# Reordering a recurrent-attention kernel with a fused feed-forward: output pieces between input pieces, preparation in three lots, one VectorE copy for two transposed tiles, input rows left in place

## The chip, the cores and the metric

The kernel runs on one core of a Trainium2 chip. A core has five engines that run their own instruction queues: TensorE (PE; its weight loads are listed apart as PEld), VectorE (DVE), ScalarE (ACT), GpSimd (POOL) and SyncE (SP, which here only issues DMA transfers). The metric is the device time of one execution in microseconds; three runs of the kernel before gave a median of 331.74 us.

## The reference

```
for t in range(S):                                   # S = 768, 4 batches, 8 heads, head size 40
    y[t]  = einsum('bhd,bhde->bhe', r[t], state)
    Sa    = einsum('bhde,bhe->bhd', state, a[t])
    state = state * w[t][:, :, None, :] - outer(Sa, b[t]) + outer(v[t], k[t])
x = y as [3072 tokens, 320]                          # all heads of a token side by side
out = (relu(x @ w_in) ** 2) @ w_out                  # 320 -> 2048 -> 320
```

A recurrence over 768 tokens for 32 (batch, head) pairs, then a feed-forward layer with squared ReLU on the result. Inputs and output are float32; the kernel computes with bf16 operands and float32 sums.

## The kernel before, in words

The 768 tokens are cut into 6 **chunks** of 128. In a chunk the 32 (batch, head) pairs are worked off in 8 **stages** of four pairs each (two heads side by side on the 128 partitions, times two), so there are 48 stages, numbered `st` = 0 to 47, and two stages share one batch of one chunk (`m` = 0 to 23). Chunks are tied by the state `UZ`, but the eight stages of a chunk are independent, so the loop is a hand-written software pipeline over `st`. There is no scheduler: each engine executes its instructions in the order in which this Python code emits them, and a wait holds everything behind it on that engine.

A stage consists of these steps (names as in the profile):

- `st_a_mm` / `st_a_ev`: PE forms two 128x128 products per pair into the PSUM banks `ca0`, `ca1`; two DVE instructions mask them into `CN`.
- `st_p` / `st_m`: PE forms `P` (from the state `UZ` and from `CN`), ACT copies it to `Mc`. Then two corrections on PE, `st_corr` (both on the line of the matmuls `P<-Mc,CN` and `P<-c,CN`), with DVE's `c` between them (`st_c1`). `st_sn` on ACT writes the result Sa into `EVX` (called Sn below; in the profile `EVX<-P`), then squares `CN` for a norm (`jk`); POOL adds up `x` and `Cc` for a later check.
- `st_t`: PE transposes Sa, and the state of the stage two back, into one PSUM tile `tb`; DVE copies the first half to `SnT`, ACT the second half to `UBD`.
- `st_ex_mm` / `st_ex_ev`: in the next stage PE forms `ex0`, `ex1` from `RV` and `SnT`; two DVE instructions mask them into `EVX`.
- `st_z`, `st_kb`: PE forms `uy` from `UBD` and from `EVX` with K and B; `st_y`, two stages on, writes the output `YS` and the new state `UZ` on DVE.

**Preparation of a batch `m`** is spread over earlier stages by a table of (stage offset, lot): `prep_cast` (ACT's Ln of w, three POOL casts), `prep_decay` (PE's running sum `cs`, two ACT exponentials `GI` and `Gp`, the products K and B with `GI` on POOL), `prep_rv`, `prep_kb`, `prep_ga` (eight PE transposes each into a PSUM tile `t`, then copies out: `RV` and `KBT` on ACT; `GT` on ACT and from it `AT` on DVE). `load` issues six DMA transfers per batch on SP; four batches fit into the buffers.

**The feed-forward** is cut in pieces that fill PE between the steps. Half a chunk (256 tokens) gives eight input pieces (`ffn_in`: six matmuls `hp`, ReLU on ACT to `hs`, the square `Gt` on DVE or POOL) and four output pieces (`ffn_out`: eight matmuls `op_`; after each second piece an ACT copy `osb` and a DMA to the output). `filler(st)` is called three times per stage and emits one waiting piece each time, so four stages take the twelve pieces of a half chunk. Before the input pieces, `gather` copies all eight heads' rows from `YS` into `X` with eight DMA transfers. After the loop, `while fill` emits what is left. At the end of each chunk two ACT squares `jm` over `Mc` and `Cc` sum the check energies.

At the very end the kernel reads a flag and would run a slow general path if the check failed.

Of the kernel before, what the change touches and what calls it, by code (L numbers as in the profile page):

```python
# [18 lines left out]
def kernel(  # L19
# [71 lines left out]
    NACC = NS + 2 * NCH + 2 * NBC  # L91
    AN, AM, AC, AG, AI = 0, NS, NS + NCH, NS + 2 * NCH, NS + 2 * NCH + NBC
# [31 lines left out]
    for key, n in (("R", 2), ("V", 2), ("A", 2), ("G", 2), ("K", 4), ("B", 4)):  # L124
        pads[key] = []
        for i in range(n):
            t_ = gl.tile([128, NHH, 64], BF16, name=f"{key}p{i}")
            nc.vector.memset(t_[:, :, D:64], 0.0)
            pads[key].append(t_)
    GTs, RVs = [], []  # L130
    for i in range(4):
        t_ = gl.tile([128, PB, L + 2], BF16, name=f"GT{i}")
        nc.vector.memset(t_[:, :, 0:1], 1.0)
        GTs.append(t_)
        t_ = gl.tile([128, 2, PB, LV], BF16, name=f"RV{i}")
        nc.vector.memset(t_[:, :, :, L:LV], 0.0)
        for s in range(2):
            o_ = 64 * s
            nc.vector.tensor_copy(
                out=t_[o_:o_ + D, 0, :, L:LV],  # L140
                in_=IDb[o_:o_ + D, o_:o_ + D].rearrange("p (u d) -> p u d", u=1)
                .to_broadcast([D, PB, D]))
        RVs.append(t_)
    EVXs = []
    for i in range(NEV):
        t_ = gl.tile([128, 2, 2, EV], BF16, name=f"EVX{i}")
        nc.vector.memset(t_[:, :, :, 2 * LV:EV], 0.0)
        EVXs.append(t_)
    UZs = []
# [14 lines left out]
    def prep_cast(m):  # L164
        o = bt[m] = Batch()
        o.R, o.A, o.G, o.V = (pads[key][m % 2] for key in "RAGV")
        o.K, o.B = (pads[key][m % 4] for key in "KB")
        o.GT, o.RV = GTs[m % 4], RVs[m % 4]
        o.EVX = [EVXs[(2 * m + u) % NEV] for u in range(2)]
        o.lnW = ffp.tile([128, NHH * D], FP32, name="lnW", tag="lnW", bufs=2)  # L170
        nc.scalar.activation(out=o.lnW[:], in_=nat.pop(("W", m))[:].rearrange("p h e -> p (h e)"),
                             func=ACTF.Ln)
        for key, pad in (("A", o.A), ("V", o.V), ("R", o.R)):
            nc.gpsimd.tensor_copy(out=pad[:, :, 0:D], in_=nat.pop((key, m))[:])

    def prep_decay(m):
# [7 lines left out]
        nc.scalar.activation(out=o.G[:, :, 0:D], in_=cs[:], func=ACTF.Exp,  # L184
                             accum_out=ACC[:, AG + m:AG + m + 1])
        for key, pad in (("K", o.K), ("B", o.B)):
            eng = nc.vector if m < 2 and key == "B" else nc.gpsimd
            eng.tensor_tensor(out=pad[:, :, 0:D], in0=nat.pop((key, m))[:], in1=GI[:],  # L188
                                    op=ALU.mult)

    def prep_load(m):
        load(m)

    def transposes(dst, pad):
        for j in range(PB):
            src = pad[:, 2 * j:2 * j + 2, :].rearrange("p a b -> p (a b)")
            nc.tensor.transpose(out=dst[:, j, :], in_=src, identity=IDb[:])  # L197

    def prep_rv(m):
        o = bt[m]  # L200
        t1 = ps.tile([128, 2, PB, L], BF16, name="t1", tag="ff", bufs=2)
        transposes(t1[:, 0], o.R)
        transposes(t1[:, 1], o.V)
        nc.scalar.activation(out=o.RV[:, :, :, 0:L], in_=t1[:], func=ACTF.Copy)  # L204
# [28 lines left out]
    CNs, Ps, SnTs, uys, Mc, Cc, YSs = {}, {}, {}, {}, {}, {}, {}  # L233
# [58 lines left out]
    def st_sn(st):  # L292
# [11 lines left out]
        if q == NQ - 1:  # L304
            for src, at in ((Mc.pop(c), AM), (Cc.pop(c), AC)):
                jm = qdp.tile([128, NQ, 4, D], BF16, name="jm", tag="jm", bufs=1)
                nc.scalar.activation(out=jm[:], in_=src[:], func=ACTF.Square,  # L307
                                     accum_out=ACC[:, at + c:at + c + 1])

    def st_t(st, su):  # L310
# [13 lines left out]
        if st < NS:  # L324
            SnT = SnTs[st] = qdp.tile([128, 2, L], BF16, name="SnT", tag="SnT")
            nc.vector.tensor_copy(out=SnT[:], in_=tb[:, 0:2])  # L326
        if 0 <= su < NS - NQ:
            nc.scalar.activation(out=UBD[:, 2 * q:2 * q + 2, :], in_=tb[:, 2:4], func=ACTF.Copy)

    exs = {}  # L330

    def st_ex_mm(st):
# [4 lines left out]
        for u in range(2):  # L337
            for i in range(2):
                for s in range(2):
                    lhsT = SnT[half(s), i, :] if u else o.RV[half(s), 1, j0 + i, 0:L]  # L340
# [4 lines left out]
    def st_ex_ev(st):
        EVX = EVXs[st % NEV]
        ex = exs.pop(st)
        for s in range(2):
            nc.vector.tensor_tensor(  # L349
                out=EVX[:, :, s, 0:2 * LV].rearrange("p i (u x) -> p i u x", u=2)[:, :, :, 0:L],  # L350
                in0=ex[s][:], in1=MEX[:].rearrange("p (i u) x -> p i u x", u=2), op=ALU.mult)

    def st_z(st):
        c, o, j0, p2, EVX = where(st)
        uy = uys[st] = ps.tile([128, 2, LV], FP32, name="uy", tag="uy")
        if c > 0:
            for i in range(2):
                nc.tensor.matmul(out=uy[:, i, :], lhsT=UBD[:, p2.start + i, :],
                                 rhs=o.RV[:, 0, j0 + i, :], start=(i == 0), stop=False,
                                 skip_group_check=True)  # L360

    def st_kb(st):
        c, o, j0, p2, EVX = where(st)
        uy = uys[st]
        for u, key in ((0, o.K), (1, o.B)):
            for i in range(2):
                for s in range(2):
                    nc.tensor.matmul(out=uy[half(s), i, :], lhsT=key[:, 2 * (j0 + i) + s, :],  # L368
# [51 lines left out]
    def ffn_in(c, hf, jj):  # L420
        flush()
# [3 lines left out]
        for u in range(2):  # L425
            j = 2 * jj + u
            for g in range(3):
                nc.tensor.matmul(out=hp[:, u, :], lhsT=WIN[g][0:rows[g], j * 128:(j + 1) * 128],  # L428
                                 rhs=Xs[c, hf][g][0:rows[g]].rearrange("p a b -> p (a b)"),
# [238 lines left out]
```

## Time and profile before

| | |
|---|---|
| median of 3 runs (range) | 331.74 us (331.05 to 333.25) |
| the profiled execution's own time | 330.49 us |
| its span (first to last instruction) | 328.8 us |
| mean granted PE clock | 0.943 of full |

The times below are microseconds from the start of that span. In timeline rows the first number is the start, the second the duration of a group of instructions, and square brackets name the idle time of the engine just before it and what ended it. Consecutive instructions of one engine overlap a little, so start-to-start distances are used where a queue is added up.

### The profile page before, as it was taken

What the parts mean: (1) busy time and instruction counts of PE and PEld (TensorE: products, weight loads), DVE (VectorE), ACT (ScalarE), POOL (GpSimd) and SP (SyncE); (2) the same over time, 40 slices, a digit from 0 to 9 for tenths busy, and PEclk for the clock granted to TensorE, in tenths of its full rate; (3) what the DMA queues carried; (4) which work ended last, traced back from release to release, by engine and by line L of the source; (5) the groups of instructions that cost most, each with busy time, mean ns of one, the idle gap of its engine ahead of it and who ended that gap; (6) DMA issues with size and microseconds to landing.
All of it is one profiled execution on the core that took longest, in us unless ns stands there. A gap on an engine that the chain in (4) does not pass through costs nothing.

```text
span 328.8 us, 10009 instructions
## 1 busy us (share of the span) xinstructions
PE 280.4 (85%) x3856; PEld 213.3 (65%) x3856; DVE 222.7 (68%) x545; ACT 232.8 (71%) x569; POOL 188.3 (57%) x342
## 2 busy tenths in 40 slices
PE   4478777799999799999799999899998899888990
PEld 3446555577777577777577777677776677666770
DVE  7226968587787587786686886686876775954430
ACT  3366766886886986887986787886887886538450
POOL 3367757296585485676476676476674673533300
PEclk9555978899999999999999999999999999999997
DMA  8992999985737437635736844735862701000100
GB/s 136 174 165 40 176 165 167 169 126 99 151 71 138 94 69 141 126 69 112 128 55 121 147 82 78 144 62 120 131 106 47 147 18 44 20 23 28 55 22 29
DMA packets 164187, 32.86 MB, mean 100 GB/s; under 512 B 158660, under 2 KB 163780, under 8 KB 164130
## 3 DMA queue, kind: packets, MB, share of 16 engines
q1 hardware_dynamic: 161586, 29.44, 49.7%
q0 software_dynamic: 2544, 2.68, 5.1%
q8 instruction: 32, 0.52, 0.7%
q14 instruction: 25, 0.20, 0.2%
HBM read 28.84 MB, written 3.93 MB: 100 GB/s over the span
## 4 chain that ended last, share of the span: by engine, by line
PE 56%; ACT 18%; issue 7%; DVE 7%; POOL 4%; DMA 3%; SPq 3%; ACTq 0%; DVEq 0%; POOLq 0%
PE hp L428 12%; PE t L197 6%; PE ex L341 4%; PE P L280 4%; PE cs L179 4%; ACT hs L433 3%; ACT jm L307 3%; PE uy L368 3%; ACT RV L204 3%; SPq L81 3%; PE tb L316 3%; PE ca L242 2%; DMA NV<-in_v_dram 2%; DVE c L288 2%; ACT GT L224 2%
## 5 line engine op out<-in xcount | busy, mean ns | idle before, releaser
L428 PE MATMUL hp<-X,WIN 120*128 120x256 bf16 (+1 forms) x576 | 78.9, 275 | 8.1 <-ACT osb L458 6.1
L433 ACT ACTIVATE hs<-hp 128x512 bf16<-128x512 f32 x96 | 57.3, 597 | 26.1 <-PE hp L428 22.7
L349 DVE TENSOR_TENSOR EVX<-ex,MEX 128x512 bf16<-128x512 f32 x96 | 61.8, 686 | 1.7 <-PE ex L341 0.5
L428 PEld LDWEIGHTS <-WIN 120*128 120x128 bf16 (+1 forms) x576 | 50.7, 98 | 18.9 <-issue 9.6
L250 DVE TENSOR_TENSOR CN<-ca,MCN 128x512 bf16<-128x512 f32 x96 | 61.4, 681 | 0.7 <-PE ca L242 0.7
L299 POOL TENSOR_TENSOR x<-Mc,c 128x160 f32<-128x160 bf16 x48 | 23.3, 486 | 66.7 <-DVE c L288 66.6
L436 POOL TENSOR_TENSOR Gt<-hs 128x512 bf16<-128x512 bf16 x43 | 48.4, 1125 | 9.9 <-ACT hs L433 9.6
L454 PEld LDWEIGHTS <-Gt 128*128 128x128 bf16 x384 | 34.3, 97 | 13.4 <-POOL Gt L436 0.8
L280 PEld LDWEIGHTS <-CN 128*128 128x128 bf16 x384 | 23.2, 98 | 27.2 <-issue 23.6
L326 DVE COPY SnT<-tb 128x256 bf16<-128x256 bf16 x48 | 14.0, 291 | 33.3 <-PE tb L322 27.6
L300 POOL TENSOR_TENSOR Cc<-x,EVX 128x160 bf16<-128x160 f32 x48 | 25.3, 527 | 17.1 <-ACT EVX L296 16.8
L436 DVE TENSOR_TENSOR Gt<-hs 128x512 bf16<-128x512 bf16 x53 | 27.4, 519 | 9.4 <-ACT hs L433 9.2
L225 DVE TENSOR_TENSOR AT<-t,GT 128x512 bf16<-128x512 bf16 x24 | 10.2, 425 | 31.4 <-ACT GT L224 31.4
L302 ACT ACTIVATE jk<-CN 128x512 bf16<-128x512 bf16 x48 | 30.1, 627 | 0.0
L212 ACT ACTIVATE KBT<-t 128x1024 bf16<-128x1024 bf16 x24 | 24.6, 1024 | 6.0 <-PE t L197 6.0
L204 ACT ACTIVATE RV<-t 128x1024 bf16<-128x1024 bf16 x24 | 24.6, 1023 | 5.1 <-PE t L197 3.0
L188 POOL TENSOR_TENSOR Kp<-NK,GI 128x320 bf16<-128x320 f32 x24 | 22.4, 933 | 6.6 <-ACT GI L182 5.6
L280 PE MATMUL P<-c,CN 128*128 128x40 bf16 x192 | 12.4, 181 | 13.5 <-DVE c L288 13.5
L288 DVE TENSOR_TENSOR c<-P,Mc 128x160 bf16<-128x160 f32 x48 | 15.3, 319 | 10.4 <-PE P L280 9.6
L378 DVE TENSOR_TENSOR YS<-uy,GT 128x256 bf16<-128x256 f32 x48 | 20.2, 421 | 1.2 <-PE uy L368 0.8
L242 PE MATMUL ca<-AT,KBT 64*128 64x128 bf16 x384 | 20.0, 228 | 1.2 <-DVE AT L225 1.2
L296 ACT ACTIVATE EVX<-P 128x160 bf16<-128x160 f32 x48 | 14.4, 300 | 8.7 <-PE P L280 8.4
(142 smaller groups left out, 636.6 us busy)
## 6 DMA issues: line engine op xcount, KB each, us to landing
NW<-in_w_dram SPq DMA_DIRECT2D x24, 160.0 KB
NK<-in_k_dram SPq DMA_DIRECT2D x24, 160.0 KB
NB<-in_b_dram SPq DMA_DIRECT2D x24, 160.0 KB
NA<-in_a_dram SPq DMA_DIRECT2D x24, 160.0 KB
NV<-in_v_dram SPq DMA_DIRECT2D x24, 160.0 KB
NR<-in_r_dram SPq DMA_DIRECT2D x24, 160.0 KB
out_dram<-osb SPq DMA_DIRECT2D x24, 160.0 KB
X<-YS SPq DMA_DIRECT2D x93, 20.0 KB
```

The source lines that it names most:

```text
L204: nc.scalar.activation(out=o.RV[:, :, :, 0:L], in_=t1[:], func=ACTF.Copy)
L212: nc.scalar.activation(out=o.KBT[:], in_=t2[:], func=ACTF.Copy)
L242: nc.tensor.matmul(out=ca[s][:, i, u, :], lhsT=o.KBT[half(s), u, j0 + i, :], rhs=o.AT[half(s), j0 + i, :], start=(i == 0 and u == 0), stop ...
L250: nc.vector.tensor_tensor(out=CN[:, :, s], in0=ca[s][:], in1=MCN[:], op=ALU.mult)
L280: nc.tensor.matmul(out=P[:, i, s, 0:D], lhsT=CN[:, i, s, 1, :], rhs=X[:, 2 * i + s], start=False, stop=last, skip_group_check=True)
L300: nc.gpsimd.tensor_tensor(out=Cc[c][:, q], in0=t_[:], in1=Sn, op=ALU.add)
L302: nc.scalar.activation(out=jk[:], in_=CN[:, :, :, 1, :], func=ACTF.Square, accum_out=ACC[:, AN + st:AN + st + 1])
L349: nc.vector.tensor_tensor(out=EVX[:, :, s, 0:2 * LV].rearrange("p i (u x) -> p i u x", u=2)[:, :, :, 0:L], in0=ex[s][:], in1=MEX[:].rearra ...
L428: nc.tensor.matmul(out=hp[:, u, :], lhsT=WIN[g][0:rows[g], j * 128:(j + 1) * 128], rhs=Xs[c, hf][g][0:rows[g]].rearrange("p a b -> p (a b) ...
L433: nc.scalar.activation(out=hs[:], in_=hp[:].rearrange("p u x -> p (u x)"), func=ACTF.Relu)
L436: later.append(lambda: eng.tensor_tensor(out=Gt[:, 2 * jj:2 * jj + 2].rearrange("p j a b -> p (j a b)"), in0=hs[:], in1=hs[:], op=ALU.mult))
L454: nc.tensor.matmul(out=op_[:], lhsT=Gts[c, hf][:, j, b_, :], rhs=WOUT[:, j, :], start=(j == 0), stop=(j == NJ - 1))
```

## The change

1. **Feed-forward order.** A half chunk's four output pieces no longer follow its own eight input pieces; they are emitted between the input pieces of the next half chunk (two outputs, four inputs, two outputs, four inputs). Pieces of a half chunk may start two stages after its gather (three before). In stages 44 and later a fourth `filler` call is made.
2. **Squares.** Of eight squares `Gt`, six go to POOL and two to DVE (four and four before); POOL's are emitted at once, not deferred.
3. **Preparation in three lots.** Ln, casts and decay of batch `m` come in stage 2m-3, K/B and G/A transposes together in stage 2m-2, R/V in stage 2m-1 (before: 2m-4, 2m-3, 2m-2). Loads are issued at 2m-9 (before 2m-7). Before the loop the work of batch 1 is cut down, K's product with `GI` comes ahead of the casts, and part of the constants is written later (`more_constants`), while three more large memsets come early.
4. **Copies.** `RV` (`RVT` now) is copied from PSUM by DVE, not ACT. `SnT` and `UBD` become one tile `TB`, copied by one DVE instruction. R/V and G/A transposes use the PSUM bank `ex0`.
5. **Order in a stage.** `st_p` comes ahead of the first filler; the two `ex` evictions are split around `c`; `st_t` comes before the decay sum and before `st_kb`.
6. **Input rows in place.** PE reads `YS` directly; only the two heads that do not fit into the first three row groups are moved, by four small DMAs (eight and a buffer `X` before). The weight `WIN` is loaded in ten pieces in this row order, over stages 1 to 3.
7. **Energies.** The two `jm` per chunk become four of half the size, in later stages.

```diff
-        t1 = ps.tile([128, 2, PB, L], BF16, name="t1", tag="ff", bufs=2)
...
-        nc.scalar.activation(out=o.RV[:, :, :, 0:L], in_=t1[:], func=ACTF.Copy)
+        t1 = turned(o.RV, tag="ex0")
+        nc.vector.tensor_copy(out=o.RVT[:, :, :, 0:L], in_=t1[:])
...
-            nc.vector.tensor_copy(out=SnT[:], in_=tb[:, 0:2])
...
-            nc.scalar.activation(out=UBD[:, 2 * q:2 * q + 2, :], in_=tb[:, 2:4], func=ACTF.Copy)
+            nc.vector.tensor_copy(out=TB[:, lo:hi], in_=tb[:, lo:hi])
...
-        eng = nc.gpsimd if jj % 2 and not tail else nc.vector
+        eng = nc.gpsimd if jj % (NJ // 4) and not tail else nc.vector
+        if jj % (NJ // 4) or tail:
+            flush()
...
+            order = outs[:2] + ins[:4] + outs[2:] + ins[4:]
...
+                ((-3, 1, prep_ln), (-3, 1, prep_cast), (-3, 4, prep_decay), (-2, 1, prep_kb),
+                 (-2, 1, prep_ga), (-1, 1, prep_rv)))
```

The loop body after the change, where the order of the steps stands:

```
        if st + 1 < NS:  st_a_mm(st + 1)
        if 1 < st <= NS: st_ex_mm(st - 1)
        if st < NS:      st_p(st); st_m(st)
        if st >= 2:      st_y(st - 2)
        if 1 <= st <= NS: st_ex_ev(st - 1, 0)
        filler(st)
        st_z(st - 1); st_corr(st, Mc, False); st_c1(st)
        st_ex_ev(st - 1, 1); st_a_ev(st + 1)
        filler(st)
        prepare(st, 1)
        st_corr(st, c1s[st], True); st_sn(st)
        filler(st)
        st_t(st, st - 2); flush()
        prepare(st, 4)
        if st >= NS - 4: filler(st)
        st_energy(st - NQ // 2)
        st_kb(st - 1)
        ...
```

Three places in the order. First ACT in the steady state, where the names are those of the steps above. Before, two stages in a row, the first with the G/A transposes (`GT`), the second with R/V and K/B:

```order
L273 ACTIVATE Mc<-P 128x160
L224 ACTIVATE GT_215<-t_2576 128x4x128
L171 ACTIVATE lnW<-NW 128x320
L433 ACTIVATE hs<-hp 128x512
L296 ACTIVATE EVX_227<-P 128x4x40
L302 ACTIVATE jk,ACC<-CN 128x512
L182 ACTIVATE GI,ACC<-cs 128x320
L184 ACTIVATE Gp_183,ACC<-cs 128x8x40
L328 ACTIVATE UBD<-tb 128x256
```

After, the stage with K/B and G/A:

```order
L275 ACTIVATE Mc<-P 128x160
L443 ACTIVATE hs<-hp 128x512 x2
L216 ACTIVATE KBT<-tt 128x1024
L226 ACTIVATE GT_190<-tt 128x4x128
L298 ACTIVATE EVX_201<-P 128x4x40
L304 ACTIVATE jk,ACC<-CN 128x512
L443 ACTIVATE hs<-hp 128x512
L314 ACTIVATE jm,ACC<-Mc 128x640
```

In the changed order two ReLUs, `KBT` and `GT` stand between `Mc` and Sn (`EVX<-P`); before, `GT`, Ln and one ReLU did. `UBD` and `RV` are gone from ACT.

Second, DVE after the change in a stage with R/V, from `c` to the first instruction of the next stage:

```order
L290 TENSOR_TENSOR c_4830<-P,Mc 128x160
L354 TENSOR_TENSOR EVX_203<-ex_4793,MEX 128x2x2x128
L252 TENSOR_TENSOR CN<-ca_4782,MCN 128x2x256
L252 TENSOR_TENSOR CN<-ca_4783,MCN 128x2x256
L210 COPY RV_195<-tt 128x8x128
L334 COPY TB<-tb 128x512
L445 TENSOR_TENSOR Gt<-hs 128x512
L383 TENSOR_TENSOR YS<-uy,GT_190 128x256
```

The copies of `RV` and of the whole `tb` now stand in DVE's queue behind the `CN` evictions; before, a copy of half of `tb` (`SnT`) stood there alone.

Third, POOL before the first stage. Before:

```order
L174 CAST Ap_179<-NA 128x8x40
L174 CAST Vp_175<-NV 128x8x40
L174 CAST Rp_171<-NR 128x8x40
L188 TENSOR_TENSOR Kp_187<-NK,GI 128x8x40
L217 COPY EVX_227<-Vp_175 128x4x40
```

After:

```order
L144 MEMSET UZ_206 128x2048
L144 MEMSET WIN_209 128x2048
L195 TENSOR_TENSOR KBp_179<-NK,GI 128x8x40
L181 CAST GAp_175<-NA 128x8x40
L181 CAST RVp_171<-NV 128x8x40
L181 CAST RVp_171<-NR 128x8x40
```

K's product (`Kp`, `KBp` now) moved ahead of the three casts, and two memsets moved ahead of it.

More of the change, by code (lines that the diff above doesn't have):

```diff
@@ L131 @@
     for i in range(4):
[L132 to L142, printed above, removed]
@@ L143 @@
-        RVs.append(t_)
-    EVXs = []
+        GTs.append(gl.tile([128, PB, L + 2], BF16, name=f"GT{i}"))
+        nc.gpsimd.memset(GTs[i][:, :, 0:1], 1.0)
+        RVs.append(gl.tile([128, 2, PB, LV], BF16, name=f"RV{i}"))
     for i in range(NEV):
[L146 to L149, printed above, removed]
+        EVXs.append(gl.tile([128, 2, 2, EV], BF16, name=f"EVX{i}"))
     for i in range(2):
         UZs.append(gl.tile([128, NP, 128], BF16, name=f"UZ{i}"))
-    UBD = gl.tile([128, NP, 128], BF16, name="UBD")
+    for g in range(PB - 1):
+        WIN.append(gl.tile([128, DFF], BF16, name=f"WIN{g}"))
@@ new lines, with more_constants @@
+    for t_, eng in ((UZs[1], nc.gpsimd), (WIN[2], nc.gpsimd), (WIN[0], nc.vector),
+                    (WIN[1], nc.vector)):
+        eng.memset(t_[:], 0.0)
+    def more_constants():
+        for t_ in RVs:
+            nc.vector.memset(t_[:, :, :, L:LV], 0.0)
+            for s in range(2):
+                o_ = 64 * s
+                nc.vector.tensor_copy(
+                    out=t_[o_:o_ + D, 0, :, L:LV],
+                    in_=IDb[o_:o_ + D, o_:o_ + D].rearrange("p (u d) -> p u d", u=1)
+                    .to_broadcast([D, PB, D]))
+        for t_ in EVXs:
+            nc.vector.memset(t_[:, :, :, 2 * LV:EV], 0.0)
@@ L364, in st_kb @@
         uy = uys[st]
-        for u, key in ((0, o.K), (1, o.B)):
+        for u in range(2):
             for i in range(2):
                 for s in range(2):
-                    nc.tensor.matmul(out=uy[half(s), i, :], lhsT=key[:, 2 * (j0 + i) + s, :],
+                    nc.tensor.matmul(out=uy[half(s), i, :], lhsT=o.KB[:, u, 2 * (j0 + i) + s, :],
                                      rhs=EVX[:, i, s, LV * u:LV * u + LV],
@@ L510 @@
         filler(st)
+        prepare(st, 1)
         if st < NS:
@@ L622, in general @@
                 for j in range(NJ):
-                    for g in range(3):
-                        nc.tensor.matmul(out=hp[:], lhsT=WIN[g][0:rows[g], j * 128:(j + 1) * 128],
-                                         rhs=xT[0:rows[g], g, :], start=(g == 0), stop=(g == 2))
+                    for g in range(NG):
+                        nc.tensor.matmul(out=hp[:], lhsT=WIN[g][:, j * 128:(j + 1) * 128],
+                                         rhs=xT[:, g, :], start=(g == 0), stop=(g == NG - 1))
                     nc.scalar.activation(out=hs[:], in_=hp[:], func=ACTF.Relu)
```

253 lines of the change are left out of this document (135 added, 118 removed).

## The prediction

> **What bounds the kernel now.** I read the page's busy shares first, then one chunk in the table by stretches, then PE's timeline.
>
> ```profile
> PE 280.4 (85%) x3856; PEld 213.3 (65%) x3856; DVE 222.7 (68%) x545; ACT 232.8 (71%) x569; POOL 188.3 (57%) x342
> ...
> 118.00:166.00 48.00, 44.45 (x652) 34.08 (x652) 35.71 (x85) 38.52 (x97) 31.02 (x57) 1.00 0.57 105
> ...
> 20.16 0.61 PE L242 MATMUL ca<-AT,KBT 64*128 64x128 bf16 x8
> ...
> 67.76 0.39 PE L242 MATMUL ca<-AT,KBT 64*128 64x128 bf16 x8
> ...
> 270.99 0.39 PE L242 MATMUL ca<-AT,KBT 64*128 64x128 bf16 x8
> ```
>
> The second row is one chunk (PE, PEld, DVE, ACT, POOL busy, then clock, DMA share, GB/s): of 48 us PE is busy 44.5, ACT 38.5, DVE 35.7, POOL 31.0, at full clock. The `ca` group opens every stage. Stage 0 opens at 20.16, stage 9 at 67.76, stage 43 at 270.99: start-up, then 34 steady stages at 203.23 / 34 = **5.98 us**, then 57.8 us of tail. PE looks full, but its ends are modelled; one stage in rows shows what it waits for:
>
> ```profile
> 217.41 0.83 PE L428 MATMUL hp<-X,WIN 120*128 120x256 bf16 x6
> ...
> 218.09 0.31 PE L358 MATMUL uy<-RV,UBD 128*128 128x168 bf16 x2
> 218.24 0.23 PE L258 MATMUL P<-UZ,AT 128*128 128x80 bf16 x2
> ...
> 218.35 0.60 ACT L433 ACTIVATE hs<-hp 128x512 bf16<-128x512 f32 x1 [0.43 <-PE hp L428]
> ...
> 218.41 0.38 PE L197 MATMUL t<-IDb,Gp 128*128 128x128 bf16 x4
> ...
> 218.84 0.30 ACT L273 ACTIVATE Mc<-P 128x160 bf16<-128x160 f32 x1
> ...
> 219.05 0.60 ACT L224 ACTIVATE GT<-t 128x512 bf16<-128x512 bf16 x1
> ...
> 219.19 0.25 PE L280 MATMUL P<-Mc,CN 128*128 128x40 bf16 x4 [0.17 <-ACT Mc L273]
> 219.29 0.82 PE L428 MATMUL hp<-X,WIN 120*128 120x256 bf16 x6
> ...
> 219.54 0.46 ACT L171 ACTIVATE lnW<-NW 128x320 f32<-128x320 f32 x1
> 219.68 0.42 DVE L225 TENSOR_TENSOR AT<-t,GT 128x512 bf16<-128x512 bf16 x1 [0.51 <-ACT GT L224]
> ...
> 220.39 0.25 PE L280 MATMUL P<-c,CN 128*128 128x40 bf16 x4 [0.28 <-DVE c L288]
> ...
> 220.49 1.25 PE L454 MATMUL op__4844<-WOUT,Gt 128*128 128x320 bf16 x8
> 220.70 0.30 ACT L296 ACTIVATE EVX<-P 128x160 bf16<-128x160 f32 x1
> ...
> 222.21 0.30 PE L316 MATMUL tb<-IDb,EVX 128*64 128x128 bf16 x4
> ...
> 222.67 0.29 DVE L326 COPY SnT<-tb 128x256 bf16<-128x256 bf16 x1 [0.76 <-PE tb L322]
> ...
> 223.46 1.26 PE L454 MATMUL op__4844<-WOUT,Gt 128*128 128x320 bf16 x8
> ```
>
> Start to start, PE itself needs 0.68 for an input piece (217.41 to 218.09), 0.15 for z, 0.17 for P (218.24 to 218.41), 0.10 for a correction, and 1.25 for the state transposes, `kb`, `ex` and `ca` (222.21 to 223.46). The rest here is waiting: `Mc` stands on ACT behind a ReLU, `c` on DVE behind `AT`, which stands behind `GT` on ACT. So the stage is PE work plus in-order queues of ACT and DVE. Prices of the other PE work come from the chain of waits, an output piece, the decay sum and eight transposes:
>
> ```profile
> 220.65 1.09 PE op__4844 L454 x8
> 221.74 0.54 PE cs L179 x2
> ...
> 215.79 0.45 PE t L197 x8
> ```
>
> **Part 1: what is removed and moved, steady state.** PE's work per pair of stages is the same before and after, since only order and places change: 2 x (0.15 + 0.17 + 0.20 + 1.25) + 3 x 0.45 + 0.54 + four input and two output pieces (2.72 + 2.18) = 10.33, or 5.2 per stage. That is the floor, 0.8 below 5.98. What the edits do to the queues:
>
> ```profile
> L204 ACT ACTIVATE RV<-t 128x1024 bf16<-128x1024 bf16 x24 | 24.6, 1023 | 5.1 <-PE t L197 3.0
> L328 ACT ACTIVATE UBD<-tb 128x256 bf16<-128x256 bf16 x40 | 15.7, 391 | 0.0
> L326 DVE COPY SnT<-tb 128x256 bf16<-128x256 bf16 x48 | 14.0, 291 | 33.3 <-PE tb L322 27.6 <-PE tb L316 5.3
> L225 DVE TENSOR_TENSOR AT<-t,GT 128x512 bf16<-128x512 bf16 x24 | 10.2, 425 | 31.4 <-ACT GT L224 31.4
> L436 POOL TENSOR_TENSOR Gt<-hs 128x512 bf16<-128x512 bf16 x43 | 48.4, 1125 | 9.9 <-ACT hs L433 9.6
> L436 DVE TENSOR_TENSOR Gt<-hs 128x512 bf16<-128x512 bf16 x53 | 27.4, 519 | 9.4 <-ACT hs L433 9.2
> L454 PEld LDWEIGHTS <-Gt 128*128 128x128 bf16 x384 | 34.3, 97 | 13.4 <-POOL Gt L436 0.8
> ```
>
> ACT loses 24.6 + 15.7 = 40 us. DVE gains a 1024-column copy 24 times: 256 columns take 291 ns and 512 bf16 from PSUM 425, so 0.13 per 256 columns gives 0.69; the bound from above is ACT's 1.02 for the same copy, from below 0.5. The larger `TB` adds 0.13 per stage, and one DVE square per pair goes (0.52). DVE stays near 37.4 of a chunk, under PE's 41. POOL takes that square at 1.125: 31.0 + 4.5 = 35.5 a chunk. Output pieces that no longer follow their own squares gain almost nothing alone: in the last row PE waited 0.8 us in all for POOL's `Gt`. What interleaving does is mix: before, a stage of three outputs ran full and a stage of three inputs waited.
>
> [...]
>
> What ends last now? I walk the two kinds of stage with the distances above, zero being the first filler. **K/B + G/A stage** (three input pieces): PE 0.68, z and correction to 0.93, second piece to 1.61, sixteen transposes to 2.51, correction, third piece to 3.29. ACT: ReLU at 0.94 (217.41 to 218.35), second ReLU at 1.87, free at 2.36 (0.49 as from 218.35 to 218.84), `KBT` about 0.95 to 3.3, `GT` 0.49 (219.05 to 219.54) to 3.8, then Sn; the state transpose follows 0.35 later (as 218.84 to 219.19) at 4.15. PE has stood 0.86 idle: **Sn behind KBT and GT on ACT is the new last wait.** Plus 1.25 and 0.17: 5.57. **R/V stage** (two outputs, one input): 1.09 + 0.25 + 1.09 + 0.45 + 0.10 + 0.68 = 3.66; Sn stands behind `osb` and Ln until about 3.5, so the transpose starts at 3.85; plus 1.25, `cs` 0.54, P 0.17: 5.8. `RV` and `TB` on DVE end just before `ex` needs them. Half-sized `jm` behind `Gp` delays `Mc` by about 0.3 in one stage of four. Together (5.57 + 5.8 + 0.15) / 2 = 5.76; with the roundings 5.75. Gain 34 x 0.23 = **8 us**; the ends are the floor of 5.2 (27 us) and a step back of 0.2 (-7).
>
> **Part 2: start-up, stages 0 to 9.**
>
> ```profile
> 5.49 0.44 ACT L182 ACTIVATE GI<-cs 128x320 f32<-128x320 f32 x1 [1.16 <-DVE RV L136]
> ...
> 8.83 0.86 POOL L188 TENSOR_TENSOR Kp<-NK,GI 128x320 bf16<-128x320 f32 x1
> ...
> 58.41 1.26 ACT L307 ACTIVATE jm<-Mc 128x1280 bf16<-128x1280 bf16 x1
> ...
> 61.07 0.60 PE L428 MATMUL hp<-X,WIN 80*128 80x256 bf16 x4 [1.11 <-DMA X<-YS]
> ...
> 64.72 0.45 POOL L174 CAST Ap<-NA 128x320 bf16<-128x320 f32 x1 [5.63 <-DMA NA<-in_a_dram]
> ```
>
> `GI` ends at 5.93 but K's product starts at 8.83, behind three casts that wait for loads; ahead of them it starts near 6.4 behind the moved memsets, 2.4 earlier. Much of batch 1's preparation leaves the path to stage 0, whose opening I put near 14 instead of 20.16. Most of that is given back: batch 1's transposes, `KBT`, `GT` and `AT` now stand inside stage 0, the G/A tile holds the bank of `ex0`, and stages 0 to 2 become about 1 us longer each. From the first `jm` at 58.41 to the opening of stage 9 at 67.76 over 9 us passed (the `jm` pair, 1.11 for `X`, and POOL's 5.63 for a load): loads two stages earlier, four gather DMAs for eight and half-sized `jm` should take 2 to 3 off. On SP the gather still queues behind a load, and the ten `WIN` transfers cost POOL issue time in stages 1 to 3, when no squares run; I count both as nothing, 2 us if the first pieces wait. Net **-5**, between -1 and -9.
>
> **Part 3: tail.**
>
> ```profile
> 301.04 0.31 PE L368 MATMUL uy<-EVX,Bp 128*64 128x168 bf16 x4
> ...
> 320.07 0.44 ACT L458 ACTIVATE osb<-op__6773 128x320 f32<-128x320 f32 x1 [1.74 <-PE op__6773 L454]
> ```
>
> From the last `kb` to the last `osb` 19.0 us pass before. After, four inputs, four outputs, eight inputs and four outputs follow it: 12 x 0.68 + 8 x 1.09 = 16.9, plus about 1.6 until POOL has three squares done and 0.6 for `osb`: 19.1. The stages ahead of it carry 20 pieces for 18, which costs about 1. The moved rows' DMAs are hidden by the four outputs. **+1.**
>
> **Sum.** The profiled execution took 330.49 us (span 328.8): 330.49 - 8 - 5 + 1 = **318.5**. The runs' median, 331.74, is 1.25 above that profile. What a measurement of this kernel can tell from no change is about 1%, 3.3 us.
>
> **Rivals.**
> - *ACT's relief reaches PE* (0.2). ACT lost 40 us; if the ReLUs start earlier than walked, Sn is not late and a stage sits near 5.3: 34 x 0.68 = 23, so 330.5 - 23 - 5 + 1 = 303.5. For it: the 31.4 us that `AT` waited for `GT`. Against: `KBT` and `GT` sit together ahead of Sn.
> - *It doesn't do what it says* (0.14). The 0.8 us on `Gt` was no cost, and the K/B + G/A stage gives back what ACT's copies leave: 5.95 to 6.0 a stage, only part of the start-up stays: about 328.
> - *POOL becomes the wait* (0.1), the slower side. K's and B's products used to have a whole stage before their transposes; now the decay sum ends one stage and the transposes stand in the middle of the next. By the walk B's product ends about 0.3 before its transpose. If one square of 1.125 is still in front of it on POOL, `KBT`, `GT`, Sn and so PE slip 0.9 a pair, and over 17 pairs the 8 us turn into about -7: 334 with half the start-up gain. It decides when POOL's work per pair, 8.9 of 11.5 us, bunches there. [...]
>
> ```profile
> 216.80 1.04 POOL L436 TENSOR_TENSOR Gt<-hs 128x512 bf16<-128x512 bf16 x1 [0.30 <-ACT hs L433]
> ```
>
> **How the numbers follow.** Forecast 0.5 (312 to 324), the three rivals 0.2, 0.14 and 0.1; 0.06 for the unforeseen, split. The range that holds 8 in 10 runs from 303 to 328.5. Faster by over 1%: 0.78; within 1%: 0.12; slower: 0.10.
>
> **What would show it.** Stage length from `ca` to `ca` near 5.75 between stages 9 and 43; PE's state transpose waiting for ACT's Sn in K/B + G/A stages only; `RV` on DVE near 0.69; ACT busy under 200 us; stage 0 opening near 14; the tail unchanged. Wrong would be: POOL's products ending after the transposes are due, DVE the engine that `ex` waits for by more than 0.3, or the first input pieces waiting for moved rows.

## Result and the profile after

The changed kernel takes **321.49 us** (median of 4 runs, 320.49 to 324.36) where the kernel before took 332.0 (4 runs, 331.05 to 333.25) beside it: a ratio of 0.9695, with a 95% interval of 0.9623 to 0.9768. The profiled execution took 320.85 us with a span of 319.2; the forecast was 318.5. The page's busy shares, the same kind of stretch as before in the table by windows (eight steady stages, in the same columns), and PE's timeline at the openings of stages 0, 9 and 43:

```profile
PE 273.6 (86%) x3856; PEld 210.2 (66%) x3856; DVE 235.9 (74%) x536; ACT 199.5 (63%) x529; POOL 209.7 (66%) x375
...
116.39:162.11 45.72, 42.96 (x651) 33.44 (x650) 37.37 (x84) 32.53 (x89) 33.69 (x60) 1.00 0.57 104
...
17.09 0.26 PE L244 MATMUL ca<-AT,KBT 64*128 64x128 bf16 x1 [1.08 <-DVE CN L252]
...
66.12 0.28 PE L244 MATMUL ca<-AT,KBT 64*128 64x128 bf16 x4
...
258.95 0.23 PE L244 MATMUL ca<-AT,KBT 64*128 64x128 bf16 x2
```

ScalarE lost 33 us, GpSimd gained 21, VectorE 13. Eight stages take 45.7 where they took 48. Cut at the openings of stages 9 and 43, the span divides as in the first two rows of this table; the other rows are the experiments below, read from their traces in the same way. The median stands beside the ratio to the kernel before, which ran on the same chip. The ratios leave out runs that fell into a slower state: one of 13 of the kernel before (438.78 us) and two of the four with `cs` moved and the memsets late (311.8 and 314.02), so that row has no ratio.

| kernel | stage 9 opens | a stage, 9 to 43 | after 43 | span | median us | ratio (95%) |
|---|---|---|---|---|---|---|
| before | 67.76 | 5.98 | 57.8 | 328.8 | 332.0 | 1 |
| **changed** | 66.12 | 5.67 | 60.2 | 319.2 | 321.49 | 0.9695 (0.9623 to 0.9768) |
| jm whole again | 66.90 | 5.93 | 62.0 | 330.4 | 333.97 | 1.0115 (1.0056 to 1.0175) |
| before, jm halved | 64.95 | 5.85 | 58.8 | 322.8 | 324.15 | 0.9788 (0.9743 to 0.9833) |
| order undone | 69.96 | 6.04 | 62.2 | 337.7 | 340.04 | 1.0282 (1.0232 to 1.0332) |
| order undone, squares 4/4 | 70.48 | 5.91 | 61.2 | 332.5 | 334.75 | 1.0132 (1.0063 to 1.0201) |
| squares 4/4 | 68.29 | 5.67 | 60.9 | 322.0 | 324.66 | 0.983 (0.9776 to 0.9883) |
| RV copy on ACT | 71.89 | 6.16 | 61.2 | 342.5 | 343.45 | 1.0376 (1.0332 to 1.0421) |
| lots undone | 75.71 | 5.76 | 57.7 | 329.4 | 330.23 | 0.9962 (0.9926 to 0.9998) |
| GT behind Sn | 67.08 | 5.59 | 59.6 | 316.8 | 321.01 | 0.9725 (0.9677 to 0.9772) |
| memsets late | 63.49 | 5.67 | 60.0 | 316.3 | 319.14 | 0.9679 (0.9621 to 0.9737) |
| cs moved | 64.29 | 5.38 | 60.4 | 307.5 | 309.56 | 0.9367 (0.9318 to 0.9416) |
| cs moved, memsets late | 63.36 | 5.38 | 59.2 | 305.3 | 309.48 | not resolved |
| the same, no fourth piece | 62.73 | 5.38 | 56.2 | 301.7 | 304.01 | 0.9193 (0.9163 to 0.9223) |

So the 9.6 us between the two spans are 1.6 at the start, 10.4 in the 34 steady stages, and 2.4 given back at the end. Of the 10.4, 1.4 are output work that is now postponed by half a chunk: stages 7 and 9 have no output pieces yet (stage 9 lasted 4.55, later R/V stages 5.95), and the tail holds what they lack. From stage 11 to 43 a stage lasts 5.71.

The first column has to be read with care, because PE's granted clock at the start was not the same in all profiles. From 8 us to the opening of stage 9 its mean was 0.72 before and 0.71 in the changed kernel, but 0.57 with the lots undone, 0.67 and 0.62 in the two kernels with the old order, and 0.97 in "before, jm halved" and "GT behind Sn". From there to the opening of stage 43 it was 1.00 in every kernel but that with the whole `jm` (0.99), so the second column is all but free of it.

A pair of steady stages in the changed kernel, as the chain of waits has it (start, length, work), from the `ca` that opens a K/B + G/A stage to the one that ends the R/V stage:

```profile
162.18 0.33 PE ca L244 x8
...
163.97 0.68 PE hp L435 x6
...
164.73 0.60 ACT hs L443
165.33 0.26 ACT KBT L216
...
166.13 0.22 ACT GT L226
...
166.60 0.33 ACT EVX L298
...
166.98 0.30 PE tb L323 x4
...
167.68 0.33 PE ca L244 x8
...
172.49 0.73 PE cs L186 x2
173.22 0.41 PE uy L373 x8
173.64 0.33 PE ca L244 x8
```

In the first half the chain leaves PE at 164.65 and runs over ScalarE (ReLU, `KBT`, `GT`, then Sn, which is the `EVX` row of L298) until `tb` at 166.98. In the second half it never leaves PE. The stage lengths are 5.5 and 5.95.

### The profile page after: what moved, and what is told of

Its sections match the earlier page's. It is cut to its first block, busy times and chain, and to the rows that moved or that the text cites. A ratio compares the mean times of both kernels' runs of the same rounds, so it can differ in the third digit from the quotient of the medians.

```text
span 319.2 us, 9845 instructions
## 1 busy us (share of the span) xinstructions
PE 273.6 (86%) x3856; PEld 210.2 (66%) x3856; DVE 235.9 (74%) x536; ACT 199.5 (63%) x529; POOL 209.7 (66%) x375
## 4 chain that ended last, share of the span: by engine, by line
PE 68%; ACT 12%; DVE 9%; issue 7%; DMA 2%; SPq 1%; POOL 0%; ACTq 0%; DVEq 0%
PE hp L435 16%; PE cs L186 5%; PE uy L373 5%; PE ca L244 5%; PE tb L323 4%; PE tt L202 4%; ACT hs L443 4%; PE ex L348 3%; ACT KBT L216 3%; PE P L282 2%; ACT EVX L298 2%; PE P L260 2%; ACT GT L226 2%; PE uy L363 2%; DMA YS<-YS 2%
## 5 line engine op out<-in xcount | busy, mean ns | idle before, releaser
L435 PE MATMUL hp<-YS,WIN 128*128 128x256 bf16 (+1 forms) x576 | 77.6, 271 | 0.7 <-DMA YS<-YS 0.7
L445 POOL TENSOR_TENSOR Gt<-hs 128x512 bf16<-128x512 bf16 x66 | 67.9, 1044 | 13.3 <-ACT hs L443 12.4
L443 ACT ACTIVATE hs<-hp 128x512 bf16<-128x512 f32 x96 | 57.7, 601 | 15.6 <-PE hp L435 13.9
L435 PEld LDWEIGHTS <-WIN 128*128 128x128 bf16 (+1 forms) x576 | 49.6, 96 | 6.9 <-issue 1.1
L195 POOL TENSOR_TENSOR KBp<-NK,GI 128x320 bf16<-128x320 f32 x24 | 20.9, 870 | 35.5 <-ACT GI L189 35.5
L301 POOL TENSOR_TENSOR x<-Mc,c 128x160 f32<-128x160 bf16 x48 | 23.5, 489 | 12.1 <-DVE c L290 11.2
L323 PE MATMUL tb<-IDb,EVX 128*64 128x128 bf16 x192 | 15.0, 238 | 18.3 <-ACT EVX L298 18.3
L216 ACT ACTIVATE KBT<-tt 128x1024 bf16<-128x1024 bf16 x24 | 24.5, 1019 | 8.2 <-PE tt L202 8.2
L275 ACT ACTIVATE Mc<-P 128x160 bf16<-128x160 f32 x48 | 14.8, 308 | 19.7 <-PE P L266 19.7
L334 DVE COPY TB<-tb 128x512 bf16<-128x512 bf16 (+1 forms) x48 | 19.0, 396 | 6.2 <-PE tb L329 4.9
L373 PE MATMUL uy<-EVX,KBp 128*64 128x168 bf16 x384 | 23.4, 246 | 0.0
L373 PEld LDWEIGHTS <-KBp 128*64 128x64 bf16 x384 | 15.0, 113 | 11.4 <-issue 11.4
```

The lines of the kernel that those rows point to most:

```text
L323: nc.tensor.transpose(out=tb[half(s), i, :], in_=EVX[:, i, s, L + LV:EV], identity=IDb[:])
L373: nc.tensor.matmul(out=uy[half(s), i, :], lhsT=o.KB[:, u, 2 * (j0 + i) + s, :], rhs=EVX[:, i, s, LV * u:LV * u + LV], start=(c == 0 and i ...
L435: nc.tensor.matmul(out=hp[:, u, :].rearrange("p (a b) -> p a b", a=HB), lhsT=WIN[g][0:ROWS[g], j * 128:(j + 1) * 128], rhs=by_pair(c, hf)[ ...
L443: nc.scalar.activation(out=hs[:], in_=flat, func=ACTF.Relu)
L445: later.append(lambda: eng.tensor_tensor(out=out_, in0=hs[:], in1=hs[:], op=ALU.mult))
```

## Experiments

### The energy squares: whole or in halves

Before the change, one stage in each chunk was long. PE's and ScalarE's timeline of the kernel before, around a chunk's end:

```profile
156.39 1.27 ACT L307 ACTIVATE jm<-Cc 128x1280 bf16<-128x1280 bf16 x1
156.50 0.28 PE L242 MATMUL ca<-AT,KBT 64*128 64x128 bf16 x4
...
158.13 0.82 PE L428 MATMUL hp<-X,WIN 120*128 120x256 bf16 x6 [1.25 <-ACT osb L458]
...
163.80 0.28 PE L242 MATMUL ca<-AT,KBT 64*128 64x128 bf16 x4
```

That stage lasted 7.30. PE waited 1.25 for a PSUM bank that `osb` had to empty, and `osb` stood behind `jm`. The twin stage half a chunk away lasted 5.62. The first run puts the whole `jm` back into the changed kernel:

```diff
             st_sn(st)
+            st_energy(st)      # whole chunk, both Mc and Cc, at q == NQ - 1
...
-        st_energy(st - NQ // 2)
```

> The two squares jm of Mc and Cc are again taken over a whole chunk in the stage that ends it, behind jk, as before the change; all else as in the changed kernel. Theory A (most of the steady gain is this split: before, one stage of every eight lasted 7.29 where its twin half a chunk away lasted 5.62, PE waiting 1.25 for osb behind jm on ScalarE, so 1.68 a chunk): 1.7 a chunk come back, 4.25 chunks between stages 9 and 43, so 7 us more, 326 to 328. Theory B (ScalarE has room since two copies left it, so jm no longer reaches PE, and the steady gain comes from those copies and the order): within 2 us of the changed kernel, which on this chip stands near 320.

The ratio to before became 1.0115: 11.2 us of span more than the changed kernel, 8.6 of it between stages 9 and 43, and all of the change's gain was gone. In the chain of waits of this kernel, just after a chunk's end:

```profile
104.65 1.26 ACT jm L313 x2
...
105.99 1.36 ACT jm L313 x2
107.35 0.49 ACT hs L442
```

2.6 us of `jm` stand ahead of a ReLU, and the stage that opens at 105.65 lasts 7.44 where its twin takes 5.46. The last of the four long stages took 8.60, with the granted clock at 0.59 from 252 to 256 us; without that the steady part is 7.4 longer. Theory A holds, also in size there; ScalarE's other relief does not hide `jm`. The second run does this part alone, in the kernel before:

```diff
-        if q == NQ - 1:
-            for src, at in ((Mc.pop(c), AM), (Cc.pop(c), AC)):
-                jm = ...                     # [128, NQ, 4, D]
...
         st_t(st, st - 2)
+        st_energy(st - NQ // 2)
```

> The kernel before with one part of the change alone: the squares jm of Mc and Cc are taken by half chunks, one in each of the two stages after the half chunk's end, as in the changed kernel. Theory (before, the whole jm made one stage of eight 7.29 long where its twin took 5.62, and putting it back into the changed kernel cost 8.7 us between stages 9 and 43): 1.4 to 1.7 a chunk go, 4.25 chunks, so 6 to 7 us less than before, near 324. Rival (the old order has other waits just behind this one): within 2 us of before, 330.

324.15 us, 0.9788 of before, as the theory had it: 6.0 us of span, 4.2 of it between stages 9 and 43 (four long stages went; stages 9 and 10 together grew by 1.5 and some others by 0.13) and 2.8 ahead of stage 9, where a long stage of 8.88 had stood, with 1.0 given back at the end. The start of this profiled execution ran at a higher granted clock, but the other three runs, whose mean clock over the whole run was 0.925 to 0.945, took 322.83 to 325.4, so the gain does not hang on it. **By the ratios this part alone gains 2.1%, where the whole change gains 3.05%: some two thirds, though the two intervals leave room for anything from under half to all of it.** In the steady stages alone the part is worth 4.2 us when it is added to the kernel before and 8.6 when it is taken from the changed one (7.4 without the lower clock), of 10.4.

### The order of the pieces, and who squares

```diff
-            order = outs[:2] + ins[:4] + outs[2:] + ins[4:]
+            order = ins + outs        # outs of the same half chunk
```

> Only the order of the pieces is undone: eight input pieces of a half chunk and then its own four output pieces, still two stages behind the gather. Theory (mixing pieces is what shortens the stages, since a stage of three inputs waits for the ReLUs and one of three outputs runs full): the steady stages go from 5.67 back to about 5.85, 6 us, the tail gives 2 back, so about 325.5. Rival (the shorter stages come from ScalarE's relief and the lots alone): stages stay at 5.7, the tail is 2 us shorter, 319 to 320.

It cost 18.5 us of span where the theory had 4 in all, 12.7 of it in the steady stages where it had 6, and the kernel was slower than before. The chain of waits of that kernel shows GpSimd where the changed kernel has none:

```profile
160.76 0.48 POOL Cc L302
161.24 1.00 POOL Gt L445
162.24 1.64 POOL KBp L195 x2
...
164.37 0.47 ACT KBT L216
```

In the old order an R/V stage can hold three input pieces. GpSimd then has squares queued ahead of the casts and of K's and B's products; a square waits for its ReLU, and the rest waits with it. The products end late, and after them the transposes, `KBT` and Sn. This is the forecast's rival "POOL becomes the wait", found in the order that the change left. A second run takes two of the six squares off GpSimd in that order, and a third does so in the changed order:

```diff
-        eng = nc.gpsimd if jj % (NJ // 4) and not tail else nc.vector
+        eng = nc.gpsimd if jj % 2 and not tail else nc.vector
```

> The order of the pieces undone, and the squares split four and four. With the order alone undone the kernel took 340.04 (before 330.21), stages 6.05 in the mean, and the chain of waits had GpSimd on 20 per cent. Theory (in the old order runs of input pieces put two to three squares of 1.04 ahead of the casts and K/B products on GpSimd, so the transposes, KBT and Sn come late; the mixed order is what lets GpSimd carry six of eight): the even split takes most of that back, stages 5.7 to 5.8, 326 to 330. Rival (the loss is PE's, stages of three inputs waiting for the ReLUs, whoever squares): the time stays at 337 to 341.

> Squares split evenly again, four on VectorE and four on GpSimd per half chunk, in the changed order. Theory (in the mixed order neither engine's squares end last): within 2 us of 320. Rival 1 (VectorE's lighter load carries the gain): VectorE's c and CN come 0.3 to 0.5 later in stages with two VectorE squares, 3 to 6 us more, 323 to 326. Rival 2 (GpSimd's K/B products end just before their transposes, so one square fewer there helps): 1 to 3 us less.

With the old order the even split takes back 5.2 of the 18.5. That is less than expected, and the rival of PE alone doesn't hold either: the chain still goes through GpSimd's casts and products. In the table of waits (us in all, times, longest) from 70 to 260 us, GpSimd's squares waited for ReLUs with the casts queued behind them, first with the old order alone, then with the even split:

```profile
POOL Gt L445 <- ACT hs L443: 36.1, 23, 3.3
...
POOL Gt L445 <- ACT hs L443: 43.4, 24, 3.2
```

In the changed kernel the same wait comes to 5.4 in that stretch, 0.3 at the longest. So fewer squares on GpSimd don't end the wait: in the old order GpSimd still stands for over 3 us behind a square whose ReLU is not there. How much of the remaining 13.3 us comes from it was not separated.

In the changed order the split leaves the steady stages as they are (192.80 us for 34, against 192.83), so neither engine's squares end last there. The time, 324.66, is rival 1's, but not for its reason: 2.2 us of the loss lie ahead of stage 9 and 0.7 at the end. Stage 7 opened 1.25 earlier there than in the changed kernel, while the moved rows came 0.7 later (59.38 against 58.69), so PE waited 2.52 for them (0.65 in the changed kernel). Their DMAs stand behind six loads on SP in both kernels and were issued at nearly the same time (50.96 against 50.83), but the small ones took 5.0 us to land in place of 3.5; why is not settled. Behind this wait PE's granted clock fell to 0.50 (62 to 64 us; 1.00 in the changed kernel), an input piece took 1.29, and stage 8 lasted 6.26 against 5.28:

```profile
59.38 0.73 PE L435 MATMUL hp<-YS,WIN 128*128 128x256 bf16 x5 [2.52 <-DMA YS<-YS]
...
63.27 1.29 PE L435 MATMUL hp<-YS,WIN 128*128 128x256 bf16 x6
...
64.51 0.82 PE L435 MATMUL hp<-YS,WIN 128*128 128x256 bf16 x6
```

The trace shows no part of this loss that the squares' engine causes. All four runs took 324.07 to 325.56, so a loss of this size comes again; that it has this cause in the runs without a trace is not shown.

### The RV copy

```diff
-        nc.vector.tensor_copy(out=o.RVT[:, :, :, 0:L], in_=t1[:])
+        nc.scalar.activation(out=o.RVT[:, :, :, 0:L], in_=t1[:], func=ACTF.Copy)
```

> The eviction of R and V (1024 columns, 24 times) goes back to ScalarE, all else as in the changed kernel. Theory (ScalarE's queue ahead of Sn sets the stage): 1.02 us more ahead of Sn or of ex in each R/V stage, of which 0.4 to 0.7 reaches PE, 17 times, so 7 to 12 us more, 329 to 333. Rival (R/V stages are bound by PE's own work, 5.95 without a wait for Sn): ScalarE has room there, VectorE is relieved by 0.68, and the time stays within 2 us of 321.5.

23 us of span more, 16.5 of it in the steady stages, more than the theory's 7 to 12: every R/V stage went from 5.95 to 6.92, the K/B + G/A stages stayed at 5.46 to 5.5. ScalarE's rows in one R/V stage:

```profile
160.69 0.44 ACT L466 ACTIVATE osb<-op__3173 128x320 f32<-128x320 f32 x1 [2.12 <-PE op__3173 L462]
161.13 1.02 ACT L210 ACTIVATE RV<-tt 128x1024 bf16<-128x1024 bf16 x1
162.05 0.46 ACT L175 ACTIVATE lnW<-NW 128x320 f32<-128x320 f32 x1
162.41 0.30 ACT L298 ACTIVATE EVX<-P 128x160 bf16<-128x160 f32 x1
```

The 1.02 of the copy stands between `osb` and Sn, and 0.97 of it reaches PE. Sn is not late in R/V stages of the changed kernel, but there is no room for a copy of 1.02 ahead of it.

### The lots of the preparation

```diff
-                ((-3, 1, prep_ln), (-3, 1, prep_cast), (-3, 4, prep_decay), (-2, 1, prep_kb),
-                 (-2, 1, prep_ga), (-1, 1, prep_rv)))
+                ((-4, 1, prep_ln), (-4, 1, prep_cast), (-4, 4, prep_decay), (-3, 1, prep_rv),
+                 (-3, 4, prep_kb), (-2, 1, prep_ga)))
```

> The lots of the preparation undone, all else as in the changed kernel: casts, Ln and decay sum two batches' stages ahead as before, R/V and K/B transposes in the odd stage, G/A transposes and cs in the even one. Theory (the new lots put 16 transposes, KBT and GT ahead of Sn in one stage and cs into the other, heavier one; moving cs alone gave 11 us): with cs in the stage that waits and KBT out of the way of Sn the pair falls from 11.43 to 10.6 to 10.9, 308 to 313. Rival 1 (KBT at the end of a stage now delays Mc and the ReLU of the next): the pair stays near 11.4, 318 to 322. Rival 2 (the lots gave the start-up gain and more): slower than the changed kernel, 323 or more.

The main theory fell. The pair takes 11.52 to 11.64 instead of 11.43 (rival 1 was nearer on this), and stage 9 opens 9.6 later, so that the time is rival 2's. Batches 1 and 2 are now both prepared inside stages 0 to 2, which last 4.9 longer. The other 4.7 fall into stages 3 to 8, and there the granted clock stood at 0.50 from 52 to 68 us, where the changed kernel had 1.00; the two causes were not separated. The kernel before prepared batch 1 ahead of stage 0, so these 9.6 are not what the lots gained over it. In the G/A stage of this kernel the chain of waits reads:

```profile
211.13 0.59 ACT GT L226
211.73 0.08 ACT lnW L175
...
211.97 0.32 ACT EVX L298
...
212.32 0.30 PE tb L323 x4
...
212.74 0.74 PE cs L186 x2
213.47 0.41 PE uy L373 x8
```

Sn is late even without `KBT` ahead of it, for Ln now stands there, and `cs` comes behind `tb`: PE waits first and does `cs` afterwards.

### The two waits that the forecast's walk had found

Sn in the K/B + G/A stage, first by taking `GT` from in front of it:

```diff
-                 (-2, 1, prep_ga)
+                 (-2, 2, prep_ga)
...
             st_corr(st, c1s[st], True)
             st_sn(st)                # Sn, x, Cc
+        prepare(st, 2)               # transposes of G and A, GT, AT
+        if st < NS:
+            st_n(st)                 # jk
```

> In K/B + G/A stages the eight transposes of G and A, GT and AT are issued behind the second correction and Sn, and jk behind GT. Theory (Sn behind KBT and GT on ScalarE is the last wait of these stages, 0.69 us of PE): the state transpose no longer waits for Sn, the stage falls from 5.48 to near 5.0, 17 times, so 8 us off, about 313. Rival (the wait only changes its name): AT comes later by what Sn comes earlier, ca of the next stage waits for it, 0.4 to 0.6 a pair come back, and the time is within 2 us of 321.5.

The wait for the most part changed its name: the K/B + G/A stage fell from 5.48 to 5.30, and `ca` now follows directly on `AT` in the chain of waits. The 2.7 us of the steady part do not show in the runs' median. Then by giving PE something to do while it waits: `cs`, which costs 0.73 at the end of the R/V stage, is put ahead of `tb` in the stage before, and Ln at the end of the stage before that:

```diff
-                ((-3, 1, prep_ln), (-3, 1, prep_cast), (-3, 4, prep_decay), ...
+                ((-5 if m > 2 else -4, 4 if m > 2 else 1, prep_ln), (-3, 1, prep_cast),
+                 (-4, 3, prep_decay), ...
...
+        prepare(st, 3)
         st_t(st, st - 2)
```

> The decay sum cs (0.73 on PE's chain) moves from the end of the R/V stage to the place in the K/B + G/A stage ahead of it where PE waits 0.69 for Sn; Ln moves half a stage ahead accordingly. Theory (R/V stages are bound by PE's own work, K/B + G/A stages by Sn on ScalarE with PE idle, so work that fits into the idle time is free): R/V stages fall from 5.95 to 5.2 to 5.4, K/B + G/A stages stay at 5.5, 0.5 to 0.7 less a pair, 17 pairs, so 9 to 12 us less, 308 to 312 where the changed kernel stands near 320. Rival (an R/V stage without cs waits for Sn or c in its turn, or the exponentials now stand ahead of Mc or KBT on ScalarE): the pair stays within 0.15 of 11.43, 318 to 322.

309.56 us, 0.9367 of before: 10.0 us less in the steady stages alone. The pair falls from 11.43 to 10.66 to 10.84, by more than the 0.73 that `cs` took on the chain where halves of `jm` don't interfere, because `kb`, which had followed it at 0.41, now takes 0.29. The chain of waits, K/B + G/A stage:

```profile
168.72 0.90 PE tt L202 x16
...
169.71 0.67 PE hp L435 x6
...
170.38 0.81 PE cs L186 x2
171.19 0.23 PE tb L323 x4
171.42 0.11 PE tb L329 x4
171.53 0.29 PE uy L373 x8
```

PE is on the chain throughout. `cs` covers Sn's lateness, and what is left is PE's own work: the forecast's floor, 10.33 a pair, was worked out with `cs` at 0.54. The edit also takes Ln from ahead of Sn in the R/V stage and brings K's and B's products a stage earlier; neither stood on the chain of the R/V stage before, which never left PE, so the gain there is that of `cs` and `kb`.

### The start and the end

GpSimd's two memsets of 1.81 us ran beside VectorE's `MCN`. They are now issued behind batch 1's casts:

```diff
-    for t_, eng in ((UZs[1], nc.gpsimd), (WIN[2], nc.gpsimd), (WIN[0], nc.vector),
-                    (WIN[1], nc.vector)):
-        eng.memset(t_[:], 0.0)
+    for t_ in (WIN[0], WIN[1]):
+        nc.vector.memset(t_[:], 0.0)
...
     prep_cast(1)
+    for t_ in (UZs[1], WIN[2]):
+        nc.gpsimd.memset(t_[:], 0.0)
```

> GpSimd's two memsets of 1.81 us (UZ, WIN) are issued behind batch 1's casts instead of ahead of K's product. Theory (they slow VectorE's MCN from 0.36 to 3.73 us, and B's product, the transposes and the first ca stand behind it): MCN back under 0.5 us, B's product near 6.7 instead of 9.97, the first ca near 10.4 instead of 13.18, and 2 to 3 us off the whole, 318.5 to 319.5. Rival (the start is set by something behind it, the constants and the waits inside stage 0): MCN is short again, the first ca is earlier, but stages 1 to 9 open as now and the time stays at 321.5. Third way: the memsets now slow CN or the EVX copies of stage 0, and the time stays or grows by 1.

The changed kernel's timeline of GpSimd and VectorE, then this one's:

```profile
2.51 3.73 DVE L121 TENSOR_SCALAR MCN<-MEX 128x256 bf16<-128x256 bf16 x2 [0.74 <-POOL MEX L115]
2.55 1.81 POOL L144 MEMSET UZ<- 128x2048 bf16 x1
4.29 1.81 POOL L144 MEMSET WIN<- 128x2048 bf16 x1
...
9.97 0.42 DVE L195 TENSOR_TENSOR KBp<-NB,GI 128x320 bf16<-128x320 f32 x1
...
13.18 0.61 PE L244 MATMUL ca<-AT,KBT 64*128 64x128 bf16 x8 [1.28 <-DVE AT L227]
```

```profile
2.51 0.36 DVE L121 TENSOR_SCALAR MCN<-MEX 128x256 bf16<-128x256 bf16 x2 [0.74 <-POOL MEX L115]
...
6.59 0.48 DVE L194 TENSOR_TENSOR KBp<-NB,GI 128x320 bf16<-128x320 f32 x1
...
10.60 0.61 PE L243 MATMUL ca<-AT,KBT 64*128 64x128 bf16 x8 [1.69 <-DVE AT L226]
```

`MCN` falls from 3.73 to 0.36 (the two memsets now run from 15.20 on), B's product starts 3.4 earlier, the first `ca` and stage 9 2.6 earlier, and the median of 319.14 is where the theory had it. The profiled execution is 2.8 shorter; the ratios of the two kernels to before lie too close to show it (0.9679 and 0.9695, each uncertain by 0.006). Last, the two gains in one kernel, and that kernel without the fourth piece of the last six stages:

> The decay sum in the K/B + G/A stage (309.56 alone) together with GpSimd's two memsets behind batch 1's casts (first ca 2.6 earlier alone, profiled time 2.8 less). Theory (the two lie in different stretches, start-up and steady state): they add, 306.5 to 308. Rival (stages 1 to 9 are set by the loads, so an earlier first ca is given back there): 309 to 310.

> As the kernel with the decay sum moved and the memsets late, but without the fourth feed-forward piece that the last six stages (44 to 49) take. Theory (those stages are full of PE work, so a piece costs the same there as in the tail): within 1 us of it. Rival (in the changed kernel stage 44 lasted 6.66 with the extra piece, and the tail behind the last kb has PE idle that would take it): 1 to 3 us less.

```diff
-        if st >= NS - 4:
-            filler(st)
```

Whether the two gains add is not resolved: the four runs of the first kernel took 306.94, 307.15, 311.8 and 314.02, of which the first two would fit a sum, and its span is 2.2 below that with `cs` alone, of which 0.9 lies ahead of stage 9. Without the fourth piece the end is 3.0 us shorter, where the rival of the expectation had put it. Stage 44, which took 6.67 with the piece between `tb` and `kb` (6.66 in the changed kernel), takes 5.35. This version, **304.01 us, 0.9193 of before**, beats both kernels.

## Why the prediction was right, and where its steps were not

The time came within 3 us, and the forecast's kind of stage was there, but all three terms were off: the steady stages gained 2.4 more than forecast, the start and the tail together 4.8 less. That the sum came out so close is in part luck, and the cause of the largest term was not the one named.

- **Steady stages, -8; measured -10.4.** The walk gave 5.57 and 5.8 for the two kinds of stage; they measured 5.46 to 5.51 and 5.95. Its central reading holds: PE waits 0.69 for Sn behind `KBT` and `GT` in K/B + G/A stages (0.86 forecast), and not in R/V stages. In the table of waits of the whole run (us in all, times, longest):

```profile
PE tb L323 <- ACT EVX L298: 18.3, 27, 1.3
```

- **What failed in it is the reading of 5.98.** That mean held a stage of 7.3 in each chunk. The walk compared one ordinary stage with a mean over stages of different limits, charged the halved `jm` 0.15, and never credited the whole one that went. With `jm` halved the kernel before has 5.85. The mixing of pieces and ScalarE's relief, which were to bring the 8 us, are needed, as their undoing costs 18 and 23 us. The undone parts sum to far more than the change brings; they do not add. A likely reason is that they pay for what the same change puts in the way: six squares on GpSimd (5.2 of the 18 by the even split), K's and B's products half a stage ahead of their transposes, `KBT` and `GT` ahead of Sn. The last two were not tested for this.
- **`cs` at 0.54.** On the chain of the changed kernel it takes 0.73, and `kb` behind it 0.41 instead of 0.29. Together that is 0.31 more than the walk had; the wait of 0.19 for Sn that it put into the R/V stage (3.66 to 3.85) did not come, which leaves 0.12, and so R/V stages are 5.95 and not 5.8. The forecast took the price from a place where `tb` follows, but that doesn't explain it: in the kernel with `cs` moved `tb` follows again, and `cs` takes 0.81. What sets its price stays open.
- **Start-up, -5; measured -1.6.** K's product came at 6.36 as forecast (6.4). B's, on VectorE, was not followed up: it stood behind `MCN`, which GpSimd's moved memsets held for 3.7 us. Stage 0 opened at 17.09 instead of 14. With the memsets out of the way it opens at 14.51, and stage 9 opens at 63.49, near the forecast's 62.8. Not foreseen either, and not tested: VectorE writes the rest of the constants (`more_constants`) ahead of the first `CN`, which starts at 16.35, 2.6 after the first `ca` has ended.
- **Tail, +1; measured +2.4.** From the last `kb` to the last `osb` 19.4 us pass (19.1 forecast). The loss is ahead of it: the fourth piece, counted as work that costs the same anywhere, delays `kb` and all that follows from it, and costs 3.0 where it was left out (the kernel with `cs` moved and the memsets late).
- **Smaller terms.** `RV` on VectorE took 679 ns, 0.69 forecast. ScalarE is busy 199.5 us, under 200 as said. K's and B's products end 0.38 before their transposes (0.3 forecast), and GpSimd's rival stayed away in this order. GpSimd's squares took 1044 ns in the mean (1125 before; the single one in the row at 216.80 that the forecast shows took 1.04 us). The price of that rival was added up wrongly: 330.5 + 7 - 5 + 1 gives the 334 with the whole of the start-up gain, and with half of it, as the text says, it would be 336.

```profile
L210 DVE COPY RV<-tt 128x1024 bf16<-128x1024 bf16 x24 | 16.3, 679 | 0.0
```

## What to carry to other kernels

Divide a mean stage into its kinds before explaining it: a stage that comes once in eight can hold the gain, and neither the busy shares nor a walk through an ordinary stage shows it. Where an engine waits in one kind of stage and is full in the next, move independent work into the wait, ahead of the waiting instruction in the program; taking away the instruction ahead of it only moved the wait. When several edits come together, undo each alone and do the suspected one alone: here one small edit alone brought some two thirds of the gain, and the undoing of others cost more than the whole change brings.

## What the hardware showed unexpectedly

- Two VectorE instructions on 256 columns (`MCN`) took 3.73 us, and ended 0.14 after GpSimd's second memset did. In the kernel before, where GpSimd ran nothing beside them, and in the run with the memsets late they took 0.36. Not every VectorE instruction beside these memsets is held: in the run with the memsets late the second one (16.94 to 18.74) runs beside `CN`, which reads the PSUM tile `ca`, and the two `CN` take 1.28 as elsewhere. What makes the difference is not shown.
- The granted clock at the start differs between executions. In the tenths of the page (40 slices of 8 us), the changed kernel was at half between 8 and 40 us; the kernel with `GT` behind Sn, the second row, which starts alike, was not:

```profile
PEclk9555589999999999999999999999999999999997
```

```profile
PEclk9999999799999999999999999999999999999996
```

  In the second, stage 5 opened 2.2 earlier (43.98 against 46.20), but stage 7 lasted 8.65 against 5.37, PE waiting 2.58 for the moved rows, which came at 58.36 (58.69 in the changed kernel). The clock fell to 0.50 behind that wait (60 to 62 us), and stage 9 opened later: the earlier stage only waited longer here. The matmuls follow the two rows only in part: up to 30 us the eight of `ca`, where no wait parts them, took 0.61 to 0.66 in both kernels, though the second row has a 9 there; from 34.93 on they took 0.40 in the second, and still 0.61 at 41.39 in the changed kernel.
